# A fused retention and relu-squared MLP kernel: the weights' way into SBUF changed, and the small matmuls of a unit given other places among the wide ones

## The chip, the cores and the metric

The kernel runs on one core of one Trainium2 chip. The metric is the device time of one execution in microseconds (us). The kernel before takes 392.28 us, the median of 3 runs from 391.2 to 393.03.

## What is computed

q, k and v are fp32 arrays of 8 batches, 8 heads, 576 positions and 64 elements. The attention is a retention: scores are not put through a softmax but multiplied by a decay that depends on head and distance. Its output, laid out as 4608 tokens of 512, goes through two weight matrices with a squared relu between them.

```python
scores = scale * np.matmul(q, k.transpose(0, 1, 3, 2))
gamma = 1.0 - 2.0 ** (-5.0 - np.arange(H, dtype=np.float32))
Dmat = np.where(rel >= 0, gamma[:, None, None] ** rel[None, :, :], 0.0)   # rel = i - j
attn = np.matmul(scores * Dmat[None], v)
x = attn.transpose(0, 2, 1, 3).reshape(B * S, H * D)      # 4608 x 512
h = x @ w_in                                              # w_in 512 x 2048
out = (np.maximum(h, 0.0) ** 2) @ w_out                   # w_out 2048 x 512
```

## The kernel before, in words

**Units and groups.** The tokens are cut into 36 units of 128: of each pair of batches, four full units of the one, four of the other, and one tail unit that holds the last 64 positions of both. Four units make a group, so there are 9 groups of 512 tokens.

**A unit's work (retention).** `load(u)` issues three DMAs on SP's queue (q, k, v, 256 KB each, fp32, in rows of 256 bytes; L68, or six halves at L71 for a tail). The pool `ld` holds five units. `cast_unit(u)` has GpSimd cast k and q to fp16 (L160, L161) and multiply v by a decay into `vp` (L164). `steps_T` is eight 128x128 transposes on TensorE into one PSUM tile `psT` (L180), followed by two copies of kT on ScalarE (L185, L186) and one of qT on VectorE (L187). `steps_score` is eight small matmuls into `psc` (L204), each four followed by VectorE's multiply with the causal mask into `rT` (L207). `steps_state` is four small matmuls (L229) that carry the state R along a batch by two VectorE operations (L238, L239; one, L235, in a batch's first unit; none in a tail). `steps_out` is eight to sixteen small matmuls (L257, L263) into `psO`, followed by VectorE's multiply into the group's `xT` (L270). `psT`, `psS` and `psO` have one PSUM buffer each, `psc` two.

**A group's work (MLP).** `steps_ff1(g)` is 16 blocks of 4 wide matmuls (128x512, L290) into `ph`; after each block ScalarE takes the relu into `rl` (L295, three buffers) and VectorE squares it into `gT` (L296). `steps_ff2(g)` is 4 token tiles of 16 wide matmuls each (L310) into `po`; after each tile ScalarE copies to `o` (L314, two buffers) and issues the store (L317, L321). `ph` and `po` share three PSUM buffers.

**Order.** The scheduling is manual: each engine executes its instructions in the order in which the program emits them. First the loads of units 0 to 3 are issued on SP's queue, and beside them eight DMAs on GpSimd's queue that load the fp32 weights and cast them to fp16 on the way (L82, L85), ahead of GpSimd's constants (ident, iota, masks; L90 to L114). VectorE's constants (L99 to L149) wait for the iota. Units 0 to 3 run one after another (L330 to L335). Then, for each group g, its 128 wide matmuls are emitted one by one, with the small steps of the four units of group g+1 put between them from a queue: 32 wide matmuls make a unit's slot, and at given phases of the slot the unit's steps are put into the queue. At phase 0 come the unit's load and casts, at 2 its transposes, at 14 scores and state, at 27 the output products; one step leaves the queue after each wide matmul, up to three from phase 27 on. The last group has no units beside it.

Of the kernel before, what the change touches and what calls it, by code (L numbers as in the profile page):

```python
# [8 lines left out]
FP32 = mybir.dt.float32  # L9
# [6 lines left out]
def kernel(  # L16
# [27 lines left out]
    NG = NU // UPG  # L44

    const = ctx.enter_context(tc.tile_pool(name="const", bufs=1))
    ld = ctx.enter_context(tc.tile_pool(name="ld", bufs=5))
    cast = ctx.enter_context(tc.tile_pool(name="cast", bufs=3))
    work = ctx.enter_context(tc.tile_pool(name="work", bufs=2))
    st_pool = ctx.enter_context(tc.tile_pool(name="st", bufs=4))  # L50
# [11 lines left out]
    def load(u):  # L62
        kind, b, c = units[u]
        t = {}
        for name, src in (("q", q), ("k", k), ("v", v)):
            x = ld.tile([P, H, D], FP32, name=f"{name}32", tag=f"{name}32")
            if kind == "full":
                nc.sync.dma_start(out=x, in_=src[b, :, c * P:(c + 1) * P, :].rearrange("h p d -> p h d"))  # L68
            else:
                for i in range(2):  # L70
                    nc.sync.dma_start(out=x[i * 64:(i + 1) * 64],  # L71
                                      in_=src[b + i, :, 512:576, :].rearrange("h p d -> p h d"))
            t[name] = x
        loaded[u] = t

    w_in16 = const.tile([P, NP, DFF], FP16, name="w_in16")
    w_out16 = const.tile([P, NF, DM], FP16, name="w_out16")

    for u in range(4):
        load(u)  # L80
    for fb in range(4):
        nc.gpsimd.dma_start(out=w_in16[:, :, fb * 512:(fb + 1) * 512],  # L82
                            in_=w_in[:, fb * 512:(fb + 1) * 512].rearrange("(m p) f -> p m f", p=P))
    for fb in range(4):
        nc.gpsimd.dma_start(out=w_out16[:, fb * 4:(fb + 1) * 4, :],  # L85
                            in_=w_out[fb * 512:(fb + 1) * 512, :].rearrange("(n p) m -> p n m", p=P))


    ident = const.tile([P, P], FP16, name="ident")
# [65 lines left out]
    def cast_unit(u):  # L155
        kind = units[u][0]
        t = loaded.pop(u)
        k16 = cast.tile([P, H * D], FP16, name="k16", tag="k16")
        q16 = cast.tile([P, H * D], FP16, name="q16", tag="q16")
        nc.gpsimd.tensor_copy(out=k16, in_=t["k"].rearrange("p h d -> p (h d)"))  # L160
        nc.gpsimd.tensor_copy(out=q16, in_=t["q"].rearrange("p h d -> p (h d)"))  # L161
        vp = vps[u % NB]
        vo = vp.rearrange("p n (a d) -> p n a d", d=64)[:, :, 0:3:2, :]
        nc.gpsimd.tensor_tensor(  # L164
            out=vo,
            in0=t["v"].rearrange("p (n a) d -> p n a d", a=2),
            in1=vdec[kind].rearrange("p (n a o) -> p n a o", a=2, o=1).to_broadcast([P, NP, 2, D]),
            op=ALU.mult)
        ret[u] = {"k16": k16, "q16": q16, "vp": vp}

    def steps_T(u):
        r = ret[u]
        steps = []
        for i, src in enumerate(("k16", "q16")):
            for hp in range(NP):
                def f(i=i, src=src, hp=hp):
                    if i == 0 and hp == 0:
                        r["psT"] = ps_one.tile([P, 2, NP, P], FP16, name="psT", tag="psT")
                    ps = r["psT"]
                    nc.tensor.transpose(ps[:, i, hp, :], r[src][:, hp * P:(hp + 1) * P], ident)  # L180
                    if hp == NP - 1:
                        if i == 1:
                            kT = kTs[u % NB]
                            qT = work.tile([P, NP, P], FP16, name="qT", tag="qT")
                            nc.scalar.copy(out=kT[0:64, :, 0, :], in_=ps[0:64, 0])  # L185
                            nc.scalar.copy(out=kT[64:128, :, 1, :], in_=ps[64:128, 0])  # L186
                            nc.vector.tensor_copy(out=qT, in_=ps[:, 1])  # L187
                            r["kT"], r["qT"] = kT, qT
                steps.append(f)
        return steps  # L190
# [109 lines left out]
    def steps_ff2(g):  # L300
        gT = gTs[g]
        steps = []
        cur = {}
        for t in range(UPG):
            kind, b, c = units[g * UPG + t]
            for f in range(NF):
                def s(t=t, f=f, kind=kind, b=b, c=c):
                    if f == 0:
                        cur["po"] = ps_ff.tile([P, DM], FP32, name="po", tag="ff")
                    nc.tensor.matmul(cur["po"], lhsT=gT[f][:, t * P:(t + 1) * P], rhs=w_out16[:, f, :],  # L310
                                     start=(f == 0), stop=(f == NF - 1))
                    if f == NF - 1:
                        o = work.tile([P, DM], FP32, name="o", tag="o")
                        nc.scalar.copy(out=o, in_=cur["po"])  # L314
                        if kind == "full":
                            r0 = b * S + c * P
                            nc.scalar.dma_start(out=out[r0:r0 + P, :], in_=o)  # L317
                        else:
                            for i in range(2):
                                r0 = (b + i) * S + 512  # L320
                                nc.scalar.dma_start(out=out[r0:r0 + 64, :], in_=o[i * 64:(i + 1) * 64])  # L321
                steps.append(s)
        return steps


    def run(steps):
        for s in steps:
            s()

    for u in range(UPG):  # L330
        cast_unit(u)
        run(steps_T(u))
        run(steps_score(u))
        run(steps_state(u))
        run(steps_out(u))  # L335

    for g in range(NG):
        nxt = [u for u in range((g + 1) * UPG, (g + 2) * UPG) if u < NU]
        wide = 2 * NF * UPG
        per = wide // UPG  # L340
        w_steps = steps_ff1(g)
        w2 = None
        queue = []
        for i in range(wide):
            if i == NF * NP:
                w_steps += steps_ff2(g)
            slot, ph = divmod(i, per)
            if nxt:
                if ph == 0:
                    u = nxt[slot]  # L350
                    load(u)
                    cast_unit(u)
                if ph == 2:
                    queue += steps_T(nxt[slot])
                if ph == 14:
                    queue += steps_score(nxt[slot])
                    queue += steps_state(nxt[slot])
                if ph == 27:
                    queue += steps_out(nxt[slot])
            w_steps[i]()  # L360
            if queue:
                queue.pop(0)()
            if ph >= 27 and queue:
                queue.pop(0)()
                if queue:
                    queue.pop(0)()
        run(queue)
# [30 lines left out]
```

## Time and profile before

| what | value |
|---|---|
| median of the runs | 392.28 us |
| the profiled execution's own time | 392.92 us |
| its span, first to last instruction | 391.2 us |
| mean granted TensorE clock | 0.997 |
| wide matmuls of the first layer, L290 | 576, 157.1 us busy |
| wide matmuls of the second layer, L310 | 576, 154.4 us busy |
| HBM read / written | 36.70 MB / 9.44 MB |

The profile counts an engine as busy while one of its instructions executes; matmuls overlap, so a matmul's shown duration is longer than the pitch at which matmuls follow one another. In the time line a row gives the start in us, the duration, the engine, the line, the operation and its tiles, and in brackets how long the engine had been idle and what ended that. PE is TensorE, PEld its weight loads, DVE VectorE, ACT ScalarE, POOL GpSimd; SPq, ACTq and POOLq are the queues on which DMAs are issued. In a group's row, "| busy, mean" are the total us and the mean ns of one.

### The profile page before, as it was taken

The page shows a single profiled execution, that of the slowest core. Times are in us where ns is not written, and L with a number is a line of the kernel's source. Part 1 is how long each engine was busy: PE and PEld are TensorE (multiplying, and loading weights), DVE is VectorE, ACT ScalarE, POOL GpSimd, SP SyncE. Part 2 cuts the span into 40 slices and gives each one's busy share as a digit, 9 for nine tenths or more (in the row PEclk, how much of TensorE's full clock was granted, in tenths as well). Part 3 has the DMA queues.
Part 4 walks back from the last instruction along what each step waited for, and adds up shares of the span by engine and source line. Part 5 has one row for each costly group of instructions (what it writes and reads, how often), then busy time and mean ns, then how long its engine had stood idle before and what let it go on. Part 6 is the DMA issues. An engine that isn't in the chain of part 4 may idle for free.

```text
span 391.2 us, 5966 instructions
## 1 busy us (share of the span) xinstructions
PE 327.6 (84%) x2272; PEld 181.1 (46%) x2272; DVE 204.5 (52%) x385; ACT 151.7 (39%) x259; POOL 92.8 (24%) x129
## 2 busy tenths in 40 slices
PE   0304699998999899989989998999899989998995
PEld 0203645554555455545545554555455545554442
DVE  1604737645654585458445844684378437633410
ACT  2102146325622562266225622662265236523721
POOL 8113632223132122222222222222222222000000
PEclk9999999999999999999999999999999999999998
DMA  8999999856145435546154455347330110011002
GB/s 146 196 196 213 208 217 219 192 137 162 28 107 136 107 83 107 136 108 136 54 139 104 82 112 148 94 86 166 90 89 2 54 55 0 2 54 56 0 31 78
DMA packets 122013, 42.34 MB, mean 108 GB/s; under 512 B 113280, under 2 KB 117376, under 8 KB 121984
## 3 DMA queue, kind: packets, MB, share of 16 engines
q1 hardware_dynamic: 112512, 28.32, 36.9%
q10 hardware_dynamic: 5248, 9.44, 7.1%
q0 software_dynamic: 4224, 4.19, 6.5%
q8 instruction: 18, 0.29, 0.3%
q14 instruction: 11, 0.09, 0.1%
HBM read 36.70 MB, written 9.44 MB: 118 GB/s over the span
## 4 chain that ended last, share of the span: by engine, by line
PE 64%; DVE 11%; ACT 10%; DMA 7%; issue 4%; SPq 3%; POOL 0%; ACTq 0%
PE ph L290 25%; PE po L310 24%; DMA v<-in_v_dram 6%; PE psc L204 5%; ACT kTb L186 5%; DVE qT L187 4%; ACT rl L295 4%; PE psO L257 4%; PE psT L180 3%; SPq L68 3%; DVE gT L296 2%; PE psS L229 2%; DVE R L239 2%; DMA out_dram<-o 2%; DVE xT L270 2%
## 5 line engine op out<-in xcount | busy, mean ns | idle before, releaser
L290 PE MATMUL ph<-xT,w_in 128*128 128x512 f16 x576 | 157.1, 383 | 5.5 <-DVE xT L270 5.5
L310 PE MATMUL po<-w_out,gT 128*128 128x512 f16 x576 | 154.4, 379 | 0.0
L295 ACT ACTIVATE rl<-ph 128x512 f16<-128x512 f32 x144 | 86.0, 597 | 72.8 <-PE ph L290 53.8
L296 DVE TENSOR_TENSOR gT<-rl 128x512 f16<-128x512 f16 x144 | 72.7, 509 | 47.3 <-ACT rl L295 44.8
L290 PEld LDWEIGHTS <-w_in 128*128 128x128 f16 x576 | 55.0, 99 | 76.1 <-issue 25.4
L310 PEld LDWEIGHTS <-gT 128*128 128x128 f16 x576 | 54.4, 98 | 68.0 <-issue 14.9
L204 PE MATMUL psc<-qT,kTb 128*128 128x128 f16 x288 | 60.0, 228 | 30.8 <-DVE qT L187 30.8
L160 POOL CAST k<-k 128x512 f16<-128x512 f32 x36 | 24.9, 691 | 199.4 <-issue 146.1
L314 ACT COPY o<-po 128x512 f32<-128x512 f32 x36 | 21.1, 585 | 91.9 <-PE po L310 87.8
L207 DVE TENSOR_TENSOR rT<-psc,mask_full 128x512 f16<-128x512 f32 x64 | 43.6, 687 | 24.0 <-PE psc L204 24.0
L187 DVE COPY qT<-psT 128x512 f16<-128x512 f16 x36 | 15.2, 423 | 68.8 <-ACT kTb L186 68.8
L180 PE MATMUL psT<-ident,k 128*128 128x128 f16 x144 | 30.9, 232 | 20.1 <-POOL k L160 20.1
L185 ACT COPY kTb<-psT 64x512 f16<-64x512 f16 x36 | 20.8, 578 | 62.4 <-PE psT L180 56.2
L164 POOL TENSOR_TENSOR vp<-v,vdec_full 128x512 f16<-128x512 f32 x32 | 34.9, 1090 | 34.2 <-PE psO L257 18.2
L257 PE MATMUL psO<-rT,vp 128*128 128x128 f16 x288 | 39.9, 229 | 0.0
L257 PEld LDWEIGHTS <-vp 128*128 128x128 f16 x288 | 28.1, 103 | 18.1 <-issue 0.3
L204 PEld LDWEIGHTS <-kTb 128*128 128x128 f16 x288 | 28.3, 102 | 14.4 <-issue 4.8
L180 PE MATMUL psT<-ident,q 128*128 128x128 f16 x144 | 30.9, 232 | 0.0
L229 PE MATMUL psS<-vp,k 128*128 128x128 f16 x128 | 27.0, 230 | 2.6 <-POOL vp L164 2.6
L263 PE MATMUL psO<-qT,R 128*128 128x128 f16 (+1 forms) x128 | 26.8, 221 | 0.0
L180 PEld LDWEIGHTS <-k 128*128 128x128 f16 x144 | 14.3, 104 | 24.3 <-POOL k L160 20.3
L239 DVE TENSOR_TENSOR R<-stmp,bdec 128x512 f16<-128x512 f32 x24 | 23.0, 960 | 0.8
(46 smaller groups left out, 157.6 us busy)
## 6 DMA issues: line engine op xcount, KB each, us to landing
q<-in_q_dram SPq DMA_DIRECT2D x32, 256.0 KB, 3.2
k<-in_k_dram SPq DMA_DIRECT2D x32, 256.0 KB, 4.2
v<-in_v_dram SPq DMA_DIRECT2D x32, 256.0 KB, 4.2
out_dram<-o ACTq DMA_DIRECT2D x32, 256.0 KB, 2.7
w_in<-in_moe_w_in_dram POOLq DMA_DIRECT2D x4, 512.0 KB, 12.6
w_out<-in_moe_w_out_dram POOLq DMA_DIRECT2D x4, 512.0 KB, 23.1
q<-in_q_dram SPq DMA_DIRECT2D x8, 128.0 KB, 3.5
k<-in_k_dram SPq DMA_DIRECT2D x8, 128.0 KB, 4.0
```

Of the source, the lines that this page charges most:

```text
L164: nc.gpsimd.tensor_tensor(out=vo, in0=t["v"].rearrange("p (n a) d -> p n a d", a=2), in1=vdec[kind].rearrange("p (n a o) -> p n a o", a=2, ...
L180: nc.tensor.transpose(ps[:, i, hp, :], r[src][:, hp * P:(hp + 1) * P], ident)
L187: nc.vector.tensor_copy(out=qT, in_=ps[:, 1])
L204: nc.tensor.matmul(r["psc"][:, hp % 2, a, :], lhsT=r["kT"][:, hp, a, :], rhs=r["qT"][:, hp, :], start=True, stop=True)
L207: nc.vector.tensor_tensor(out=rT[:, hp - 1:hp + 1].rearrange("p n a i -> p (n a) i"), in0=r["psc"].rearrange("p n a i -> p (n a) i"), in1= ...
L229: nc.tensor.matmul(ps[:, hp], lhsT=r["k16"][:, hp * P:(hp + 1) * P], rhs=vo, start=True, stop=True)
L239: nc.vector.tensor_tensor(out=Rn, in0=tmp, in1=bdec, op=ALU.mult)
L257: nc.tensor.matmul(r["psO"][:, hp, :], lhsT=r["vp"][:, hp, a * 64:a * 64 + P], rhs=r["rT"][:, hp, a, :], start=(a == 0), stop=(a == 1 and ...
L290: nc.tensor.matmul(cur["ph"], lhsT=w_in16[:, m, f * P:(f + 1) * P], rhs=xTs[g][:, m, :], start=(m == 0), stop=(m == NP - 1))
L295: nc.scalar.activation(out=rl, in_=cur["ph"], func=ACTF.Relu)
L296: nc.vector.tensor_tensor(out=gT[f], in0=rl, in1=rl, op=ALU.mult)
L310: nc.tensor.matmul(cur["po"], lhsT=gT[f][:, t * P:(t + 1) * P], rhs=w_out16[:, f, :], start=(f == 0), stop=(f == NF - 1))
```

## The change

The weights are loaded as fp32 on SP's queue, into four staging buffers of 1 MB: the four pieces of w_in behind the loads of units 0 to 3; each piece of w_out when VectorE has cast the piece of w_in that held its buffer. VectorE casts w_in between units 0 to 3 and group 0, and w_out between the matmuls of group 0's second layer. Loads of units 4 to 9 follow the weights on SP's queue; the pool `ld` holds six units, and later loads are issued six units ahead. For units 0 to 7 VectorE casts q instead of GpSimd.

Group 0's wide matmuls now run with no units between them, its second layer with three token tiles side by side and the fourth behind them. Units 4 to 7 run one after another behind group 0. From group 1 on the small steps stand between the wide ones as before, at other places: in the slot of unit u its state comes at phase 0, its scores at 5, the transposes of unit u+1 at 14, the output products of u at 18; one step leaves the queue after each wide matmul, two from phase 14 on. GpSimd's casts are emitted a slot earlier, for u+1. Unit 8, the first, also has its own transposes in its slot, and its steps come 8 phases later.

```diff
--- before.py
+++ after.py
@@ -44,7 +44,8 @@
     NG = NU // UPG
 
     const = ctx.enter_context(tc.tile_pool(name="const", bufs=1))
-    ld = ctx.enter_context(tc.tile_pool(name="ld", bufs=5))
+    ld = ctx.enter_context(tc.tile_pool(name="ld", bufs=6))
+    stage = ctx.enter_context(tc.tile_pool(name="stage", bufs=4))
     cast = ctx.enter_context(tc.tile_pool(name="cast", bufs=3))
     work = ctx.enter_context(tc.tile_pool(name="work", bufs=2))
     st_pool = ctx.enter_context(tc.tile_pool(name="st", bufs=4))
@@ -73,17 +74,27 @@
             t[name] = x
         loaded[u] = t
 
+
     w_in16 = const.tile([P, NP, DFF], FP16, name="w_in16")
     w_out16 = const.tile([P, NF, DM], FP16, name="w_out16")
-
-    for u in range(4):
+    NLD = 6
+    for u in range(UPG):
         load(u)
+    w_st = []
     for fb in range(4):
-        nc.gpsimd.dma_start(out=w_in16[:, :, fb * 512:(fb + 1) * 512],
-                            in_=w_in[:, fb * 512:(fb + 1) * 512].rearrange("(m p) f -> p m f", p=P))
-    for fb in range(4):
-        nc.gpsimd.dma_start(out=w_out16[:, fb * 4:(fb + 1) * 4, :],
-                            in_=w_out[fb * 512:(fb + 1) * 512, :].rearrange("(n p) m -> p n m", p=P))
+        t = stage.tile([P, NP, 512], FP32, name=f"wi{fb}", tag="wst")
+        nc.sync.dma_start(out=t, in_=w_in[:, fb * 512:(fb + 1) * 512].rearrange("(m p) f -> p m f", p=P))
+        w_st.append(t)
+
+    def load_w_out(fb):
+        t = stage.tile([P, 4, DM], FP32, name=f"wo{fb}", tag="wst")
+        nc.sync.dma_start(out=t, in_=w_out[fb * 512:(fb + 1) * 512, :].rearrange("(n p) m -> p n m", p=P))
+        w_st.append(t)
+
+    def cast_w(i):
+        fb = i % 4
+        dst = w_in16[:, :, fb * 512:(fb + 1) * 512] if i < 4 else w_out16[:, fb * 4:(fb + 1) * 4, :]
+        nc.vector.tensor_copy(out=dst, in_=w_st[i])
 
 
     ident = const.tile([P, P], FP16, name="ident")
@@ -158,7 +169,7 @@
         k16 = cast.tile([P, H * D], FP16, name="k16", tag="k16")
         q16 = cast.tile([P, H * D], FP16, name="q16", tag="q16")
         nc.gpsimd.tensor_copy(out=k16, in_=t["k"].rearrange("p h d -> p (h d)"))
-        nc.gpsimd.tensor_copy(out=q16, in_=t["q"].rearrange("p h d -> p (h d)"))
+        (nc.vector if u < 2 * UPG else nc.gpsimd).tensor_copy(out=q16, in_=t["q"].rearrange("p h d -> p (h d)"))
         vp = vps[u % NB]
         vo = vp.rearrange("p n (a d) -> p n a d", d=64)[:, :, 0:3:2, :]
         nc.gpsimd.tensor_tensor(
@@ -300,26 +311,31 @@
     def steps_ff2(g):
         gT = gTs[g]
         steps = []
-        cur = {}
-        for t in range(UPG):
+        po = {}
+
+        order = [(t, f) for t in range(UPG) for f in range(NF)] if g else \
+                [(t, f) for f in range(NF) for t in range(3)] + [(3, f) for f in range(NF)]
+        for t, f in order:
             kind, b, c = units[g * UPG + t]
-            for f in range(NF):
-                def s(t=t, f=f, kind=kind, b=b, c=c):
-                    if f == 0:
-                        cur["po"] = ps_ff.tile([P, DM], FP32, name="po", tag="ff")
-                    nc.tensor.matmul(cur["po"], lhsT=gT[f][:, t * P:(t + 1) * P], rhs=w_out16[:, f, :],
-                                     start=(f == 0), stop=(f == NF - 1))
-                    if f == NF - 1:
-                        o = work.tile([P, DM], FP32, name="o", tag="o")
-                        nc.scalar.copy(out=o, in_=cur["po"])
-                        if kind == "full":
-                            r0 = b * S + c * P
-                            nc.scalar.dma_start(out=out[r0:r0 + P, :], in_=o)
-                        else:
-                            for i in range(2):
-                                r0 = (b + i) * S + 512
-                                nc.scalar.dma_start(out=out[r0:r0 + 64, :], in_=o[i * 64:(i + 1) * 64])
-                steps.append(s)
+
+            def s(t=t, f=f, kind=kind, b=b, c=c):
+                if g == 0 and t == 0 and f % 4 == 0:
+                    cast_w(4 + f // 4)
+                if f == 0:
+                    po[t] = ps_ff.tile([P, DM], FP32, name="po", tag="ff")
+                nc.tensor.matmul(po[t], lhsT=gT[f][:, t * P:(t + 1) * P], rhs=w_out16[:, f, :],
+                                 start=(f == 0), stop=(f == NF - 1))
+                if f == NF - 1:
+                    o = work.tile([P, DM], FP32, name="o", tag="o")
+                    nc.scalar.copy(out=o, in_=po[t])
+                    if kind == "full":
+                        r0 = b * S + c * P
+                        nc.scalar.dma_start(out=out[r0:r0 + P, :], in_=o)
+                    else:
+                        for i in range(2):
+                            r0 = (b + i) * S + 512
+                            nc.scalar.dma_start(out=out[r0:r0 + 64, :], in_=o[i * 64:(i + 1) * 64])
+            steps.append(s)
         return steps
 
 
@@ -327,41 +343,57 @@
         for s in steps:
             s()
 
-    for u in range(UPG):
+    def whole(u):
         cast_unit(u)
+        if u + NLD < NU and u >= UPG:
+            load(u + NLD)
         run(steps_T(u))
         run(steps_score(u))
         run(steps_state(u))
         run(steps_out(u))
 
-    for g in range(NG):
-        nxt = [u for u in range((g + 1) * UPG, (g + 2) * UPG) if u < NU]
-        wide = 2 * NF * UPG
-        per = wide // UPG
+    for u in range(UPG):
+        whole(u)
+    for i in range(4):
+        cast_w(i)
+        load_w_out(i)
+    for u in range(UPG, UPG + NLD):
+        load(u)
+    run(steps_ff1(0))
+    run(steps_ff2(0))
+    for u in range(UPG, 2 * UPG):
+        whole(u)
+
+
+    SLOT = 2 * NF
+    for g in range(1, NG):
         w_steps = steps_ff1(g)
-        w2 = None
         queue = []
-        for i in range(wide):
+        for i in range(NF * NP * 2):
             if i == NF * NP:
                 w_steps += steps_ff2(g)
-            slot, ph = divmod(i, per)
-            if nxt:
+            slot, ph = divmod(i, SLOT)
+            u = (g + 1) * UPG + slot
+            late = 8 if u == 2 * UPG else 0
+            if u < NU:
                 if ph == 0:
-                    u = nxt[slot]
-                    load(u)
-                    cast_unit(u)
-                if ph == 2:
-                    queue += steps_T(nxt[slot])
-                if ph == 14:
-                    queue += steps_score(nxt[slot])
-                    queue += steps_state(nxt[slot])
-                if ph == 27:
-                    queue += steps_out(nxt[slot])
+                    if late:
+                        cast_unit(u)
+                        queue += steps_T(u)
+                    if u + 1 < NU:
+                        cast_unit(u + 1)
+                    if u + NLD < NU:
+                        load(u + NLD)
+                if ph == late:
+                    queue += steps_state(u)
+                if ph == late + 5:
+                    queue += steps_score(u)
+                if ph == late + 14 and u + 1 < NU:
+                    queue += steps_T(u + 1)
+                if ph == late + 18:
+                    queue += steps_out(u)
             w_steps[i]()
-            if queue:
-                queue.pop(0)()
-            if ph >= 27 and queue:
-                queue.pop(0)()
+            for _ in range(2 if ph >= 14 else 1):
                 if queue:
                     queue.pop(0)()
         run(queue)
```

## The prediction

> **What bounds the kernel now.** I read the page's busy times and slices first, then TensorE's waits after the first group, then the time line.
>
> ```profile
> span 391.2 us, 5966 instructions
> ...
> PE 327.6 (84%) x2272; PEld 181.1 (46%) x2272; DVE 204.5 (52%) x385; ACT 151.7 (39%) x259; POOL 92.8 (24%) x129
> ...
> PE   0304699998999899989989998999899989998995
> ```
>
> TensorE is nearly full from slice 6 on and nearly empty in the first five slices (each 9.8 us). So there are two places to gain or lose: an opening of some 50 us, and the tenth that is missing afterwards. What is missing afterwards has two names:
>
> ```profile
> PE psc L204 <- DVE qT L187: 18.2, 28, 0.7
> PE ph L290 <- DVE xT L270: 4.3, 8, 0.8
> ```
>
> These are TensorE's waits between 90 and 391 us (total us, times, longest): 28 waits, one for each unit 8 to 35, and 8 at the starts of groups 1 to 8. TensorE waits for nothing else there. One of them, in the time line (start, us):
>
> ```profile
> 207.85 1.24 PE L290 MATMUL ph<-xT,w_in 128*128 128x512 f16 x5
> 209.75 0.22 PE L204 MATMUL psc<-qT,kTb 128*128 128x128 f16 x1 [0.65 <-DVE qT L187]
> 209.80 0.38 PE L290 MATMUL ph<-xT,w_in 128*128 128x512 f16 x1
> 210.07 0.38 PE L290 MATMUL ph<-xT,w_in 128*128 128x512 f16 x1
> ```
>
> A wide matmul is shown with 0.38 us, but five take 1.24, so the pitch is (1.24 - 0.38) / 4 = 0.215. One wide and one small take 0.27 (209.80 to 210.07), so a small one takes 0.055. The five from 207.85 are issued by 208.93, and the next starts at 209.75: the wait costs 0.82, its shown 0.65 and the pipeline's tail of 0.165. The transposes are followed by 5 wide matmuls (1.1 us), while the copies out of their PSUM tile take longer than that.
>
> ```profile
> 49.02:90.11 41.09, 37.91 (x252) 20.33 (x252) 23.74 (x39) 16.47 (x28) 11.97 (x16) 1.00 0.98 181
> 90.11:128.42 38.31, 35.13 (x252) 19.20 (x252) 21.09 (x37) 16.53 (x29) 9.70 (x13) 1.00 0.45 111
> 205.25:224.26 19.01, 17.70 (x129) 9.82 (x128) 13.19 (x25) 11.33 (x20) 4.25 (x6) 1.00 0.44 97
> 358.92 13.97 PE L290 MATMUL ph<-xT,w_in 128*128 128x512 f16 x64 [0.78 <-DVE xT L270]
> ```
>
> The first three rows are windows (length, then busy time of PE, weight loads, DVE, ACT, POOL): group 0, group 1, and the two slots of first-layer work in group 4. The last row starts group 8. Groups 1 to 7 take 358.92 - 90.11 = 268.8 us, 38.4 each; their pure issue is 128 x 0.215 + 124 x 0.055 = 34.3.
>
> **Steady groups.** Transposes of unit u+1 now go out at phase 14 of slot u, two per step, and its scores at phase 5 of its own slot, 23 steps later. The wait for qT ends. Scores finish at phase 12, the output products run from 18 to about 25, so xT is ready some 6 wide matmuls (1.3 us) before the group ends, against 0.69 for its multiply: the boundary wait ends too. Saved in groups 1 to 7: 28 x 0.82 = 23.0, and 4.3 - 0.57 (the one at 90.11) + 7 x 0.165 = 4.9, together 27.9; 240.9 remain, 34.4 a group. What is late next: between the last score and the first output product lie 6 wide and some 8 small matmuls, 1.7 us, in which VectorE must do the second mask multiply (0.69) behind a gT that waits for ScalarE. In the first-layer half VectorE has 13.19 us of work for two slots that shrink from 19.0 to 17.2, 77%, so queues can form; I allow 1.0 in all. Unit 8, which has no slot ahead of it, still waits 8 to 13 steps, slow ones, as group 1 starts; no cost. Loads six units ahead instead of being issued in the unit's own slot sit on SP's queue and cost nothing: a group used DMA at 0.45.
>
> **The start.** GpSimd loses eight DMA issues:
>
> ```profile
> 1.32 3.16 POOL L82 DMA_DIRECT2D w_in<-in_moe_w_in_dram  x4 [0.80 <-POOLq L382]
> 4.43 3.01 POOL L85 DMA_DIRECT2D w_out<-in_moe_w_out_dram  x4
> 7.35 0.30 POOL masks.py:197 MEMSET ident<- 128x128 f16 x1
> 8.14 0.15 DVE L117 COPY iota_pt<-iota_p 64x1 f32<-64x1 f32 x1 [6.20 <-POOL iota_p L92]
> ...
> 15.38 0.27 DVE L149 MEMSET kTb<- 64x256 uint32 x1
> ...
> 15.98 1.01 PE L204 MATMUL psc<-qT,kTb 128*128 128x128 f16 x8 [4.67 <-DVE qT L187]
> ...
> 18.64 0.69 DVE L270 TENSOR_TENSOR xT<-psO,gam_full 128x512 f16<-128x512 f32 x1
> ```
>
> Ident can start at 1.32 instead of 7.35, and VectorE's constants, which wait for the iota, end 6.03 earlier, at 15.65 - 6.03 = 9.62. Now the serial units, here unit 2 into unit 3:
>
> ```profile
> 39.54 1.01 PE L204 MATMUL psc<-qT,kTb 128*128 128x128 f16 x8 [1.73 <-DVE qT L187]
> ...
> 42.57 0.63 PE L180 MATMUL psT<-ident,q 128*128 128x128 f16 x4
> ...
> 42.69 0.68 DVE L270 TENSOR_TENSOR xT<-psO,gam_full 128x512 f16<-128x512 f32 x1
> ...
> 43.30 0.58 ACT L185 COPY kTb<-psT 64x512 f16<-64x512 f16 x1 [4.26 <-PE psT L180]
> ...
> 44.99 1.01 PE L204 MATMUL psc<-qT,kTb 128*128 128x128 f16 x8 [1.79 <-DVE qT L187]
> ```
>
> Scores to scores took 5.45. The q cast of units 0 to 7 moves from GpSimd to VectorE, where in program order it stands behind xT of the unit before; the q transposes wait for it. New period: 39.54 to the end of xT at 43.37 is 3.83, the cast, then transposes to scores 42.57 to 44.99 = 2.42 (+0.05 to start). For VectorE's casts the trace has a copy of 1 element at 0.15 (L117) and one of 256, and a multiply that converts 512:
>
> ```profile
> 10.56 0.29 DVE L130 COPY gam_tail<-gam_full 128x256 f32<-128x256 f32 x1 [1.56 <-ACT gam_full L129]
> ...
> L207 DVE TENSOR_TENSOR rT<-psc,mask_full 128x512 f16<-128x512 f32 x64 | 43.6, 687 | 24.0 <-PE psc L204 24.0
> ```
>
> The copies give 0.15 + 0.00055 per element: 0.43 for q's 512, 1.28 for 2048 of a weight piece. The other bound is the multiply's 0.687 per 512: 0.69 and 2.75. I take the copies, which are the same operation. Period 3.83 + 0.43 + 2.47 = 6.73. Scores(0) start at 9.62 + 0.43 + 2.47 = 12.5; unit 0 needs 3.35 to the end of xT (15.98 to 19.33); scores(1) at 12.5 + 3.35 + 2.90 = 18.8, scores(3) at 32.2, xT(3) done at 36.1; before, the first wide matmul, which waits for it, started at 49.02 (row below). Data is there in time:
>
> ```profile
> q1 hardware_dynamic: 112512, 28.32, 36.9%
> q10 hardware_dynamic: 5248, 9.44, 7.1%
> ```
>
> The unit loads (252 bytes a packet) need 36.9% of 391.2 for 28.32 MB: 196 GB/s, 4.0 us a unit. The output queue (1.8 KB a packet) makes 340 GB/s; for the weights' 2 KB rows that is 3.1 us a piece, 5.4 at the unit loads' rate. Four units by 18, w_in by 30 (39 at worst); w_out's four pieces, which wait on SP for the casts to free their buffers, by 52 (61); units 4 to 9, behind them in the same queue, one each 4.0 us, unit 4 by 58 (67). None is last.
>
> **Group 0, now without units beside it.** The first cast ends at 37.4 and the first wide matmul starts. The other three hold VectorE until 41.2; six PSUM and relu buffers let TensorE run on. It starts slow:
>
> ```profile
> 49.02 1.44 PE L290 MATMUL ph<-xT,w_in 128*128 128x512 f16 x3 [1.22 <-DVE xT L270]
> ...
> 54.10 1.33 PE L290 MATMUL ph<-xT,w_in 128*128 128x512 f16 x5
> ```
>
> From 49.02 to 54.10 went 11 wide and 8 small ones, worth 2.8 us at the later pitch: 2.3 lost, although the window's granted clock reads 1.00. First layer: 37.4 + 64 x 0.215 + 2.3 = 53.5. The second layer begins only after the last relu and square and the first cast of w_out, all behind one another:
>
> ```profile
> L295 ACT ACTIVATE rl<-ph 128x512 f16<-128x512 f32 x144 | 86.0, 597 | 72.8 <-PE ph L290 53.8 <-DVE gT L296 18.6
> L296 DVE TENSOR_TENSOR gT<-rl 128x512 f16<-128x512 f16 x144 | 72.7, 509 | 47.3 <-ACT rl L295 44.8
> ...
> L314 ACT COPY o<-po 128x512 f32<-128x512 f32 x36 | 21.1, 585 | 91.9 <-PE po L310 87.8
> ...
> out_dram<-o ACTq DMA_DIRECT2D x32, 256.0 KB, 2.7
> ```
>
> Pipeline tail 0.165, relu 0.60, square 0.51, cast 1.28, hand-overs 0.1: 2.7. The later casts (1.28 each) hide behind 12 matmuls (2.6). Second layer ends at 53.5 + 2.7 + 13.8 = 70.0. Its first three output tiles finish together 3.4 us earlier, with two output buffers: the third copy waits for a store (0.585 + 2.7), the fourth for the next one, and unit 4's kT copies stand behind both on ScalarE, until about 72 instead of 70.7. So scores(4) start 1.3 late, at 70.0 + 0.44 (eight transposes at 0.055) + 1.99 (the 2.42 above without its four slow transposes, 0.43) + 1.3 = 73.7.
>
> **Units 4 to 7, now alone.** scores(5) = 73.7 + 3.35 + 2.90 = 79.9; xT(7) ends 79.9 + 2 x 6.73 + 3.83 = 97.2. Group 1 starts at 97.3, before at 90.11: the opening loses 7.2. In the serial rows above eight small matmuls take 1.01, a pitch of (1.01 - 0.22) / 7 = 0.113 against 0.055 in the stream, so TensorE is back at half rate and group 1 pays the 2.3 of a slow start, which before it did not. This agrees with the Trainium skill, "TensorE: Matmul & The Clock Gate", Part 1: the array runs at half clock until about 3.4 us of steady work and falls back after an idle window of that length. It speaks against this change, since units 4 to 7 running alone buy a second slow start; without the rule group 1 would start warm and the sum below would be 372.7.
>
> **Sum.** 97.3 + 2.3 + 240.9 + 1.0 + group 8 with the last store, unchanged, 391.2 - 358.92 = 32.3: span 373.8, against 391.2. The profiled execution took 392.92, 1.72 more than its span, and the median of the runs is 392.28, 0.64 less: 373.8 + 1.1 = 374.9, say 375.
>
> **Rivals.** *The wait moves instead of going* (first-layer half): output products wait for the second mask multiply, or PSUM fills while VectorE works off its queue. For it: in-order VectorE with gT in front, 1.7 us of room against some 1.5. Against: in the second-layer half VectorE is half idle. In 14 slots 0.82 each, 11.5: 386. *The opening is cheaper*: no slow start of group 1 (2.3), no store in ScalarE's way (1.3), no residue (1.0): 370. *Slower*: the same mask multiply is late in all 28 slots and the boundary xT behind it, so that nothing of the 27.9 comes back while the opening still loses 9.5: 403. It decides for slower once under 8 of the 27.9 arrive, that is, over 0.6 us lost per slot. Against: the shown room. In between, two thirds lost: about 392, no change. That the change does not do what it says is small: the step counts above come from the code, and only tile dependencies I do not see could hold the early transposes back, which is this last rival again.
>
> **How the numbers follow.** Forecast 375: 0.70. Moved wait, 386: 0.13. Cheaper opening, 370: 0.11. Nothing regained, 403: 0.04; about 392: 0.02. Forecast's own unknowns: casts at their upper bound cost 7 x 0.26 + 2 x 1.47 + some 2 for the blocked squares, 7 together; a slow start of the second layer after its 2.7 gap 2.3. Range 367 to 387: the low end is the cheap opening with 3 for what I summed too long in the serial chain, the high end the moved wait. A difference under 0.5%, 2 us, can't be told from none. Faster 0.94, same 0.02, slower 0.04.
>
> **What would show it.** The psc wait for qT after group 1 gone from the list, groups 34.4 to 34.6 long; ident near 1.3; serial scores 6.7 apart; a VectorE cast of 1.3; a TensorE gap near 2.7 between group 0's layers; group 1 starting near 97 with a pitch near 0.43. Wrong would be groups over 36, a new name in TensorE's waits, or group 1 starting past 105.

## The result and the profile after

The changed kernel takes 374.87 us, the median of 4 runs (372.89 to 375.75), against 392.12 for the kernel before in the same comparison: a ratio of 0.9553, 95% interval 0.9504 to 0.9602. Six more runs on another occasion gave 372.72 (370.71 to 375.46), ratio 0.9516 (0.9482 to 0.9551). 375 had been forecast. The profiled execution took 375.74, its span is 374.0.

The page of the changed kernel, busy times and slices (a slice is 9.35 us; PEclk is the granted TensorE clock in tenths):

```profile
PE 332.7 (89%) x2272; PEld 186.3 (50%) x2272; DVE 207.1 (55%) x401; ACT 151.4 (40%) x259; POOL 84.1 (22%) x113
...
PE   0565979654899999999999999999999999999995
...
PEclk9986798955599999999999999999999999999999
...
GB/s 175 253 358 9 359 256 190 172 220 148 222 142 113 154 154 94 116 141 133 86 124 151 119 86 142 150 104 118 109 29 2 28 58 28 2 58 58 0 53 60
```

TensorE works earlier than before and is 90% busy or more from the twelfth slice to the last but one, but slices 8 to 10, 65 to 94 us, are half empty, and slices 9 to 11 have a granted clock of a half: mostly units 4 to 7 alone. Its waits between 100 us and the end are one row; 28 and 8 waits stood there before.

```profile
PE psc L215 <- DVE qT L198: 0.3, 1, 0.3
```

Windows of group 4 and of units 4 to 7 (length; busy time of PE, weight loads, DVE, ACT, POOL; granted clock; DMA share; GB/s):

```profile
204.08:238.63 34.55, 34.55 (x253) 19.44 (x252) 21.31 (x39) 16.54 (x28) 9.51 (x12) 1.00 0.52 123
70.65:97.36 26.71, 13.86 (x126) 11.80 (x125) 15.82 (x26) 5.23 (x9) 8.84 (x11) 0.59 1.09 202
```

Group 4 took 38.53 before and is now busy from end to end with the same matmuls. The time line, the rows at which the forecast can be checked:

```profile
0.80 0.21 POOL masks.py:197 MEMSET ident<- 128x128 f16 x1 [0.29 <-POOLq L414]
9.16 0.35 DVE L172 CAST q<-q 128x512 f16<-128x512 f32 x1
11.91 1.01 PE L215 MATMUL psc<-qT,kTb 128*128 128x128 f16 x8 [1.73 <-DVE qT L198]
17.99 1.01 PE L215 MATMUL psc<-qT,kTb 128*128 128x128 f16 x8 [1.73 <-DVE qT L198]
24.34 1.01 PE L215 MATMUL psc<-qT,kTb 128*128 128x128 f16 x8 [1.73 <-DVE qT L198]
34.30 4.62 DVE L97 CAST w_in<-wi 128x2048 f16<-128x2048 f32 x4
35.58 16.79 PE L301 MATMUL ph<-xT,w_in 128*128 128x512 f16 x64 [2.22 <-DVE w_in L97]
53.46 6.73 DVE L97 CAST w_out<-wo 128x2048 f16<-128x2048 f32 x4
54.73 12.22 PE L326 MATMUL po<-w_out,gT 128*128 128x512 f16 x48 [2.37 <-DVE w_out L97]
69.31 0.59 ACT L330 COPY o<-po 128x512 f32<-128x512 f32 x1 [1.11 <-DMA out_dram<-o]
73.54 0.61 PE L215 MATMUL psc<-qT,kTb 128*128 128x128 f16 x8 [2.28 <-DVE qT L198]
79.68 1.01 PE L215 MATMUL psc<-qT,kTb 128*128 128x128 f16 x8 [1.73 <-DVE qT L198]
97.36 0.58 PE L301 MATMUL ph<-xT,w_in 128*128 128x512 f16 x1 [1.12 <-DVE xT L281]
103.89 0.22 PE L215 MATMUL psc<-qT,kTb 128*128 128x128 f16 x1 [0.28 <-DVE qT L198]
135.20 0.38 PE L301 MATMUL ph<-xT,w_in 128*128 128x512 f16 x1
341.70 13.98 PE L301 MATMUL ph<-xT,w_in 128*128 128x512 f16 x64
```

The row at 97.36 and the last two start groups 1, 2 and 8. Groups 2 to 7 take (341.70 - 135.20) / 6 = 34.42 us, 38.4 before. Group 0's two rows hold two slow starts: 64 wide matmuls in 16.79, 2.8 more than the 13.99 that the same row takes at full pitch in a run below, and 48 in 12.22, 1.7 more than the 10.53 there. A third stands at group 1: from 97.36 to the first score at 103.89, 14 wide and 8 small matmuls worth 3.45, the wait of 0.28 and the tail of 0.165 leave 2.6 lost. (The expectations below speak of 2.1 for the second layer; 0.4 of it is a wait of the fourth token tile for a PSUM buffer.) So the time of the steady groups came back nearly whole, and the opening gave 7.25 of it away (97.36 against 90.11).

### The profile page after: what moved, and what is told of

Its sections match the earlier page's. It is cut to its first block, busy times and chain, and to the rows that moved or that the text cites. A ratio compares the mean times of both kernels' runs of the same rounds, so it can differ in the third digit from the quotient of the medians.

```text
span 374.0 us, 5968 instructions
## 1 busy us (share of the span) xinstructions
PE 332.7 (89%) x2272; PEld 186.3 (50%) x2272; DVE 207.1 (55%) x401; ACT 151.4 (40%) x259; POOL 84.1 (22%) x113
## 4 chain that ended last, share of the span: by engine, by line
PE 84%; DVE 10%; ACT 4%; issue 1%; ACTq 0%
PE ph L301 34%; PE po L326 34%; PE psc L215 5%; PE psT L191 4%; PE psO L268 4%; DVE rT L218 2%; PE psS L240 2%; ACT kTb L197 1%; ACT kTb L196 1%; DVE xT L281 1%; PE psO L274 1%; DVE R L250 1%; DVE qT L198 1%; DVE stmp L249 1%; DVE q L172 1%
## 5 line engine op out<-in xcount | busy, mean ns | idle before, releaser
L326 PE MATMUL po<-w_out,gT 128*128 128x512 f16 x576 | 150.9, 383 | 2.6 <-DVE w_out L97 2.4
L307 DVE TENSOR_TENSOR gT<-rl 128x512 f16<-128x512 f16 x144 | 67.3, 472 | 48.3 <-ACT rl L306 47.5
L215 PE MATMUL psc<-qT,kTb 128*128 128x128 f16 x288 | 55.9, 234 | 14.8 <-DVE qT L198 14.8
L175 POOL TENSOR_TENSOR vp<-v,vdec_full 128x512 f16<-128x512 f32 x32 | 36.2, 1133 | 106.6 <-PE psO L274 45.3
L171 POOL CAST k<-k 128x512 f16<-128x512 f32 x36 | 23.2, 644 | 108.9 <-DMA k<-in_k_dram 53.0
L268 PE MATMUL psO<-rT,vp 128*128 128x128 f16 x288 | 46.9, 236 | 0.6 <-DVE rT L218 0.6
L215 PEld LDWEIGHTS <-kTb 128*128 128x128 f16 x288 | 28.1, 105 | 19.3 <-ACT kTb L196 7.9
L268 PEld LDWEIGHTS <-vp 128*128 128x128 f16 x288 | 29.5, 106 | 14.9 <-issue 1.1
L191 PE MATMUL psT<-ident,q 128*128 128x128 f16 x144 | 20.3, 234 | 9.4 <-DVE q L172 9.4
L191 PE MATMUL psT<-ident,k 128*128 128x128 f16 x144 | 20.7, 238 | 6.0 <-POOL k L171 6.0
L191 PEld LDWEIGHTS <-q 128*128 128x128 f16 x144 | 13.6, 104 | 17.5 <-DVE q L172 11.1
```

The lines of the kernel that those rows point to most:

```text
L175: nc.gpsimd.tensor_tensor(out=vo, in0=t["v"].rearrange("p (n a) d -> p n a d", a=2), in1=vdec[kind].rearrange("p (n a o) -> p n a o", a=2, ...
L215: nc.tensor.matmul(r["psc"][:, hp % 2, a, :], lhsT=r["kT"][:, hp, a, :], rhs=r["qT"][:, hp, :], start=True, stop=True)
L268: nc.tensor.matmul(r["psO"][:, hp, :], lhsT=r["vp"][:, hp, a * 64:a * 64 + P], rhs=r["rT"][:, hp, a, :], start=(a == 0), stop=(a == 1 and ...
L307: nc.vector.tensor_tensor(out=gT[f], in0=rl, in1=rl, op=ALU.mult)
L326: nc.tensor.matmul(po[t], lhsT=gT[f][:, t * P:(t + 1) * P], rhs=w_out16[:, f, :], start=(f == 0), stop=(f == NF - 1))
```

## The experiments

The theory is that of the forecast: two waits end in the steady groups, for 27.9 us; the opening loses, because units 4 to 7 run alone, because VectorE's q cast stands in their chain, and because TensorE, little used there, falls to half rate. Each run takes one of these apart. Edits are shown shortened, by their main lines.

**The old slots in the new opening.** In the loop over groups 1 to 8 the steps go back to their old phases, one a wide matmul and three from phase 27 on, and the casts to the unit's own slot:

```diff
-                if ph == late: queue += steps_state(u)
-                if ph == late + 5: queue += steps_score(u)
-                if ph == late + 14 and u + 1 < NU: queue += steps_T(u + 1)
-                if ph == late + 18: queue += steps_out(u)
+                if ph == 2: queue += steps_T(u)
+                if ph == 14: queue += steps_score(u) + steps_state(u)
+                if ph == 27: queue += steps_out(u)
```

> The changed kernel with the old places of the small steps from group 1 on (transposes at phase 2, scores and state at 14, output products at 27, casts in the unit's own slot); the opening and the loads six ahead stay. If the phases are what removed the waits: 28 waits of 0.82 us and the boundary waits of 4.9 come back, groups of 38.4 instead of 34.5, time 374.9 + 27.9 = 403, slower than the kernel before by about 10, which is then what the new opening alone costs. Rival, that the loads issued further ahead removed the waits: time stays near 375.

Measured: 398.34 us, ratio to the kernel before 1.0189 (1.016 to 1.0218): about 2% slower than that. TensorE's waits over the whole execution and the first rows of groups 1 and 8:

```profile
PE psc L215 <- DVE qT L198: 32.8, 36, 2.3
...
PE ph L301 <- DVE xT L281: 4.8, 8, 1.1
```

```profile
93.41 1.44 PE L301 MATMUL ph<-xT,w_in 128*128 128x512 f16 x3 [1.08 <-DVE xT L281]
...
364.05 6.20 PE L301 MATMUL ph<-xT,w_in 128*128 128x512 f16 x28 [0.78 <-DVE xT L281]
```

Both waits are back, and groups 1 to 7 take 270.6 against 244.3 in the changed kernel: 26.3 us hang on the phases, not on the loads issued ahead. The time is 4.7 under the 403 expected, mostly because group 1 starts at 93.4 instead of 97.4 with an opening that is the same code: here the first layer's 64 matmuls took 15.58 and the second layer started at full pitch.

**The new slots behind the old opening.** The kernel before, with its loop replaced by the changed kernel's, from group 0 on:

```diff
-    for g in range(NG):            # old slots, load and casts in the unit's own slot
+    for u in range(UPG, UPG + 5):
+        load(u)
+    for g in range(NG):            # new slots; unit 4 takes the late phases, loads 5 ahead
```

> The kernel before, its opening and GpSimd's weight DMAs kept, with the new places of the small steps from group 0 on (unit 4 takes the late phases), loads five ahead. If the phases alone give the gain: 392.1 - 27.9 = 364 from groups 1 to 7, and group 0 loses four waits of 0.82 and one boundary wait of 0.73, so about 360, and the changed opening is a loss of some 14 us. Rival, that the new order needs the new opening (loads too late for transposes half a slot ahead, new TensorE waits for GpSimd's k): 370 or more.

Measured: 360.53 us, ratio 0.9227 (0.9202 to 0.9253). It is faster than the changed kernel by 12 to 14. TensorE's waits, from the serial units 0 to 3 and the start of group 0:

```profile
PE psT L180 <- POOL k L160: 19.9, 2, 10.2
PE psc L204 <- DVE qT L187: 9.9, 4, 4.7
...
PE ph L290 <- DVE xT L270: 1.3, 1, 1.3
```

So the slots, with the loads issued ahead, are worth about 30 us, and everything else in the change together is a loss.

**q cast on GpSimd.**

```diff
-        (nc.vector if u < 2 * UPG else nc.gpsimd).tensor_copy(out=q16, ...)
+        nc.gpsimd.tensor_copy(out=q16, ...)
```

> The changed kernel with q of units 0 to 7 cast on GpSimd again. If the cast on VectorE, behind xT, lengthens the chain from unit to unit: the periods fall from 6.35 (units 0 to 3) and 6.9 (units 4 to 7) to the 5.45 of the kernel before, 3 x 0.9 + 3 x 1.4 and 0.4 for unit 0, 7 us less: 368. Rival, that the cast is hidden or GpSimd becomes as late: 374 to 376.

Measured: 362.32 us, ratio 0.9265 (0.9236 to 0.9294). Its time line:

```profile
9.57 1.01 PE L215 MATMUL psc<-qT,kTb 128*128 128x128 f16 x8 [2.45 <-DVE qT L198]
...
25.32 1.01 PE L215 MATMUL psc<-qT,kTb 128*128 128x128 f16 x8 [1.79 <-DVE qT L198]
30.34 13.99 PE L301 MATMUL ph<-xT,w_in 128*128 128x512 f16 x64 [2.22 <-DVE w_in L97]
46.62 10.53 PE L326 MATMUL po<-w_out,gT 128*128 128x512 f16 x48 [2.29 <-DVE w_out L97]
64.68 0.61 PE L215 MATMUL psc<-qT,kTb 128*128 128x128 f16 x8 [3.23 <-DVE qT L198]
83.97 0.38 PE L301 MATMUL ph<-xT,w_in 128*128 128x512 f16 x1 [1.12 <-DVE xT L281]
```

From the first unit's scores to the fourth's it takes 15.75, 5.25 each, and the first layer starts 5.2 us earlier. From scores(4) to group 1 it takes 19.3 instead of 23.8, another 4.5. Together 9.7 against the 7 expected; 2 of the surplus are unit 0, whose scores start at 9.57 instead of 11.91 (0.4 had been put there), since its q cast no longer stands behind VectorE's constants. On top none of the three starts of wide matmuls in this profile is slow (64 x 0.215 and the tail make 13.93), which the changed kernel's profile pays with 2.8, 1.7 and 2.6. The q cast is the dearest single line of the change, 10 to 13 us by the medians, in which the chain's share and that of the slow starts are not told apart.

**Filler between group 0's layers.**

```diff
     run(steps_ff1(0))
+    fill = ps_ff.tile([P, UPG * P], FP32, name="fill", tag="ff")
+    for i in range(12):
+        nc.tensor.matmul(fill, lhsT=w_in16[:, 0, 0:P], rhs=xTs[0][:, 0, :], start=True, stop=True)
```

> The changed kernel with 12 wide matmuls into an unused PSUM tile between the two layers of group 0 (extra work; the result is thrown away), 2.6 us at full pitch, in the gap in which TensorE waits for the first cast of w_out. If the half rate at the second layer's start (8 matmuls at 0.43 from 54.73 on) comes from the idle gap: the pitch is 0.215 from the first matmul on, the second layer takes 13.9 instead of 15.9, time 373. Rival, that it comes from what runs beside it (VectorE's casts, DMA share 1.28): the pitch stays 0.43, time 375 or more.

Measured: 372.99 us, ratio 0.9544 (0.9517 to 0.9572), no different from the changed kernel's two sets.

```profile
35.97 13.99 PE L301 MATMUL ph<-xT,w_in 128*128 128x512 f16 x64 [2.22 <-DVE w_in L97]
49.80 2.75 PE L365 MATMUL fill<-xT,w_in 128*128 128x512 f16 x12
52.39 10.52 PE L326 MATMUL po<-w_out,gT 128*128 128x512 f16 x48
...
66.69 0.59 ACT L330 COPY o<-po 128x512 f32<-128x512 f32 x1 [2.55 <-DMA out_dram<-o]
```

The second layer runs at full pitch from its first matmul, as the idle-gap theory wants. But it also does so in the two kernels above, with gaps of 2.3 us and no filler, so this run does not settle it. And the second layer's shorter time does not come through whole: ScalarE waits 2.55 us for the first token tile's store, 1.11 in the changed kernel, as in the next run.

**w_out cast inside the first layer.**

```diff
-    run(steps_ff1(0))
+    for i, s in enumerate(steps_ff1(0)):
+        s()
+        if i in (35, 43, 51, 59):
+            cast_w(4 + (i - 35) // 8)
```

with the call in `steps_ff2` removed.

> The changed kernel with the four casts of w_out emitted among the last blocks of group 0's first layer (behind wide matmuls 36, 44, 52 and 60) instead of in its second layer. Theory: the second layer's first matmul waits only for the cast that stands behind the last relu and square; without it the gap of 2.4 goes, and with the gap the chance of a slow start (2.1 in the profiled run, none in two others): 2.4 to 4.5 less, 371 to 372.5. Rival, that the stores of the first token tiles, or the loads of units 4 and 5, end last instead: 374 to 375.

Measured: 372.13 us, ratio 0.9476 (0.944 to 0.9512). That lies within the 371 to 372.5 expected, but the interval overlaps both sets of the changed kernel, and the second set's 372.72 is only 0.6 away: a gain is not shown. The gap before the second layer is gone, and most of its time is not:

```profile
50.65 10.09 PE L324 MATMUL po<-w_out,gT 128*128 128x512 f16 x46 [0.25 <-ACT rl L306]
64.42 0.39 PE L191 MATMUL psT<-ident,k 128*128 128x128 f16 x4
69.10 1.01 PE L215 MATMUL psc<-qT,kTb 128*128 128x128 f16 x8 [4.06 <-DVE qT L198]
```

```profile
65.36 0.59 ACT L328 COPY o<-po 128x512 f32<-128x512 f32 x1 [3.40 <-DMA out_dram<-o]
```

```profile
88.84 1.01 PE L215 MATMUL psc<-qT,kTb 128*128 128x128 f16 x8 [1.79 <-DVE qT L198]
...
92.77 0.38 PE L301 MATMUL ph<-xT,w_in 128*128 128x512 f16 x1 [1.12 <-DVE xT L281]
93.03 0.38 PE L301 MATMUL ph<-xT,w_in 128*128 128x512 f16 x1
```

Unit 4's scores start 4.7 us after its first transpose, 2.9 in the changed kernel. ScalarE waits 3.40 instead of 1.11 for the first token tile's store before it can copy the third, and the kT copies stand behind that. So the rival was right for 1.8 of the 2.4. The traces bear out that the store now falls among the loads of units 4 to 9: in the 2 us in which it is issued the DMA share is 1.25 here (60 to 62 us) and 1.29 with the filler (62 to 64), where the wait is 2.55, but 0.00 in the changed kernel (66 to 68). No run moves the loads alone. The profile's span, 367.3, is 6.7 below the changed kernel's 374.0, about as much as the three slow starts there (7.1), none of which it has. Group 1 starts at full pitch at 92.77, though unit 7's eight scores before it ran at half rate (1.01), as in the changed kernel.

**Weights loaded by GpSimd as before.**

```diff
-        nc.sync.dma_start(out=t, in_=w_in[...])          # fp32, staged, cast by VectorE; w_out likewise
+    for fb in range(4):
+        nc.gpsimd.dma_start(out=w_in16[...], in_=w_in[...])
+    for fb in range(4):
+        nc.gpsimd.dma_start(out=w_out16[...], in_=w_out[...])
```

> The changed kernel with the weights loaded and cast by GpSimd's eight DMAs at the start, as in the kernel before, and no weight casts on VectorE; all else as changed. Theory: the weights' DMAs run beside the unit loads again, so unit 2's k arrives near 35 and xT of unit 3 is done near 50 instead of 34.4; the casts (1.2 before the first layer, 2.4 before the second) are saved: about 15.5 - 1.2 - 2.4 = 12 more, 387. Rival, that the bytes are the same and only the sum of them counts: 373 to 376.

Measured: 385.32 us, ratio 0.9837 (0.9802 to 0.9872), 10 to 13 more than the changed kernel.

```profile
31.33 1.01 PE L204 MATMUL psc<-qT,kTb 128*128 128x128 f16 x8 [1.73 <-DVE qT L187]
...
51.20 15.76 PE L290 MATMUL ph<-xT,w_in 128*128 128x512 f16 x64 [1.09 <-DVE xT L270]
```

Unit 1's scores are at 31.33 instead of 17.99 and the first layer starts at 51.20 instead of 35.58. That the bytes are the same does not help; units 0 to 3 need theirs first. The weights' new way is the good half of the opening.

**Units 4 to 7 back beside group 0.** The weights' new way, the new slots, q on GpSimd, and:

```diff
+    for u in range(UPG, 2 * UPG):            # on SP's queue behind w_in, ahead of w_out
+        load(u)
-    run(steps_ff1(0))
-    run(steps_ff2(0))
-    for u in range(UPG, 2 * UPG):
-        whole(u)
-    for g in range(1, NG):
+    for g in range(NG):                      # unit 4 takes the late phases
+            if g == 0 and i in (48, 58, 68, 80):
+                cast_w(4 + (48, 58, 68, 80).index(i))
```

> The changed kernel's weight path and slots, with units 4 to 7 put back between group 0's wide matmuls (unit 4 in the late phases), their loads ahead of w_out's, q always cast on GpSimd, and w_out's casts among group 0's wide matmuls. Theory, from the rows: group 0's first wide matmul at about 30.5 as with q on GpSimd, group 0 34.4 and up to 2.8 for a slow start and 1 for unit 4, group 1 warm at 67 to 69, then 7 x 34.4 + 32.3: span 340 to 342, time 342 to 345. Rival, that the loads can't feed units 5 to 7 and w_out in time, or VectorE can't do casts and units at once: TensorE waits in group 0, 350 or more.

Measured: 346.9 us, ratio 0.8858 (0.8827 to 0.8888), faster than both kernels, and 15.4 less than with q on GpSimd alone, for units 4 to 7 beside group 0 and w_out's casts moved together.

```profile
29.95 0.61 PE L303 MATMUL ph<-xT,w_in 128*128 128x512 f16 x1 [2.41 <-DVE w_in L99]
...
32.69 0.29 PE L193 MATMUL psT<-ident,k 128*128 128x128 f16 x1 [2.13 <-POOL k L173]
```

The second row, 2.13 us in which unit 4's first transpose waits because its k lands behind all of w_in, is about as long as the time is over the 345 expected; whether it is the cause the run after the next asks, and leaves open.

**Fillers in the serial units.**

```diff
+        run(ts[:4]); filler(u, 3 if u else 0)     # wide matmuls, lhsT=ident, rhs=k16, unused tile
+        run(ts[4:]); filler(u, 6)
-        run(steps_T(u))
```

> The changed kernel with extra wide matmuls on old data into an unused PSUM tile in the waits of the serial units 0 to 7 (three while q is cast, six while qT is copied; extra work, thrown away). Theory, that the half rate in and after the serial units comes from TensorE's low activity there: small matmuls at 0.055 instead of 0.11 from unit 1 or 2 on, no slow start of groups 0 and 1: 2.8 + 2.6 and about 0.5 a unit less, 365 to 370. Rival, that the half rate comes from the units' loads and copies beside it: the same 0.11, and 375 or more, since fillers at half rate delay the scores.

Measured: 372.37 us, ratio 0.9504 (0.947 to 0.9537). The small matmuls now run at full pitch:

```profile
24.13 0.61 PE L215 MATMUL psc<-qT,kTb 128*128 128x128 f16 x8 [0.43 <-DVE qT L198]
30.34 0.61 PE L215 MATMUL psc<-qT,kTb 128*128 128x128 f16 x8 [0.49 <-DVE qT L198]
...
35.17 15.67 PE L301 MATMUL ph<-xT,w_in 128*128 128x512 f16 x64 [2.57 <-DVE w_in L97]
```

```profile
68.00:96.00 28.00, 19.98 (x178) 11.87 (x176) 15.59 (x26) 5.90 (x11) 9.84 (x11) 1.00 1.04 207
```

Eight scores take 0.61, a pitch of (0.61 - 0.22) / 7 = 0.056, and the granted clock is 1.00 in the window of units 4 to 7, where the DMA share (1.04) and the copies are as before. So the half rate in the serial units is TensorE's own low activity, and the rival falls. But the time hardly does: the units' chain runs through VectorE and ScalarE and keeps a period of 6.2, and after the pause of 2.57 for w_in's cast the first layer still starts slow (1.7), although the units before it ran at full pitch. The time expected from the fillers, 365 to 370, was not reached.

**The same with another order of loads.** From the kernel of 346.9: unit 4's load behind w_in's first piece, and w_in's first cast ahead of unit 3's steps.

```diff
         w_st.append(t)
+        if fb == 0:
+            load(UPG)
...
     for u in range(UPG):
+        if u == UPG - 1:
+            cast_w(0)
         whole(u)
```

> The kernel with units 4 to 7 beside group 0 (346.9), with unit 4's load ahead of w_in's last three pieces on SP's queue, and w_in's first cast ahead of unit 3's steps on VectorE. Theory, from that kernel's waits: the 2.13 us in which unit 4's first transpose waits for GpSimd's k and the cast's 1.2 ahead of group 0's first matmul go, 3.3 less, 343.6; up to 2.3 more or less by whether TensorE starts group 0 at half rate. Rival, that w_in's later pieces or their casts then end last: 346 to 348.

Measured: 345.84 us (344.0 to 347.64), ratio 0.8846 (0.8803 to 0.8888): within the interval of the kernel that it comes from. Both waits are gone from TensorE's list, and the first ten wide matmuls of group 0 are issued at half rate, until 34.65:

```profile
29.37 0.58 PE L305 MATMUL ph<-xT,w_in 128*128 128x512 f16 x1 [1.08 <-DVE xT L285]
...
34.12 0.63 PE L305 MATMUL ph<-xT,w_in 128*128 128x512 f16 x1
...
35.06 0.38 PE L305 MATMUL ph<-xT,w_in 128*128 128x512 f16 x1
```

In this profile group 1 starts at 69.12 instead of 72.05, near the 3.3 less that was expected. But only two of the four executions are that fast (344.0 and 344.08); the other two took 347.6 and have no profile. Whether it is faster stays open.

**The changed kernel once more**, unaltered.

> The changed kernel once more, unaltered, for a second profile and more times. Theory, that its slow starts fall differently from execution to execution (in the first profile 2.8, 2.1 and 2.6 us at the three starts of wide matmuls after a pause): the same constants, periods and groups of 34.4, another set of slow starts, times spread over 2 to 3 us around 375. Rival, that they are fixed by the program: the same three slow starts of the same sizes.

Measured: 372.72 us (370.71 to 375.46). The profiled execution is again the slowest (375.46), with the same slow starts to 0.1 us:

```profile
35.59 16.75 PE L301 MATMUL ph<-xT,w_in 128*128 128x512 f16 x64 [2.22 <-DVE w_in L97]
54.63 12.22 PE L326 MATMUL po<-w_out,gT 128*128 128x512 f16 x48 [2.29 <-DVE w_out L97]
```

The other five runs have mean granted clocks of 0.954 to 0.977 instead of 0.939 and take 370.71 to 373.0. So two profiles agree, which the rival expected, and the times spread over 4.75 us, even more than the theory expected. Over both sets the three executions at a clock of 0.938 or 0.939 take 375.46 to 375.75; among the others the time does not follow the mean clock (373.0 at 0.977, 370.71 at 0.968). What decides the set of slow starts in an execution is open.

## Why the prediction was right

**Steady groups: right.** 34.42 us a group against 34.4, and the only wait left was unit 8's first (0.3). The two reversals, one each way, put the slots' worth at 26.3 (by the traces of the old slots in the new opening) and about 30 (by the medians in the old opening, where group 0 gains too, 360.5 against 360 expected). The rival in which output products wait for the second mask multiply did not come: TensorE's list has 0.6 us of it in all, within the serial units.

**The opening: the sum right, its terms less so.** Group 1 was to start at 97.3 and did at 97.36, by errors that cancel:

| step | forecast | measured |
|---|---|---|
| q cast of unit 0 can start | 9.62 | 9.16 |
| scores to scores, units 1 to 3 | 6.73 | 6.35, 6.41 |
| one cast of w_in | 1.28 | 1.15 |
| first wide matmul | 37.4 | 35.58 |
| slow start, first layer | 2.3 | 2.8 |
| gap between the layers | 2.7 | 2.5 |
| slow start, second layer | 0, bound 2.3 | 1.7 |
| fourth token tile's wait for a PSUM buffer | 0 | 0.4 |
| second layer's end to scores(4) | 3.7 | 2.9 |
| scores(4) to group 1 | 23.6 | 23.8 |
| slow start, group 1 | 2.3 | 2.6 |

The first wide matmul came 1.8 early: 0.5 because VectorE's constants ended sooner, 0.7 in the two periods from unit 1 to unit 3, whose q transposes took 0.40 instead of the 0.61 to 0.63 of half rate, and the rest in small parts of units 0 and 3 and in the cast. The second layer's slow start, put at nothing in the sum and at 2.3 among the unknowns, took 1.7; the way from the second layer's end to scores(4) was 0.8 shorter, since ScalarE waited for one store, 1.11 us, and not for two.

The 2.3 itself was read a little low: from 49.02 to 54.10 the kernel before issued 10 wide and 8 small matmuls, not 11 and 8, so 2.5 were lost. And the step from the serial units' half rate to a slow start of group 1 is not sure. The half rate in those units is TensorE's own low activity, as the fillers show, and it needs no long pause: in units 4 to 7 TensorE was busy for 13.86 of 26.71 us and never idle for more than 2.3 at a time. But two profiles, with q on GpSimd and with the early casts, have the same half rate in the units ahead of group 1 and a group 1 that starts at full pitch. So a start of wide matmuls costs between 0 and 2.8 us. The sum has two slow ones, 4.6 us; the profile of the changed kernel has three, 7.1, and those two profiles none. That 375 was met so closely is partly luck.

By the Trainium skill, "TensorE: Matmul & The Clock Gate", Part 1, the activity window is free-running, so that a start can be slow in one execution and not in another. The starts here agree in that: behind the same code the first layer's 64 matmuls lost 2.8 us in the changed kernel, 1.6 with the old slots and 0 with the filler. The two equal profiles of the unaltered kernel do not speak for chance alone. The idle window that the prediction cites from there is not seen in units 4 to 7: their half rate came with pauses of at most 2.3 us.

**Data in time: right.** The page's third slice, in which the pieces of w_in are on their way, shows 358 GB/s for their 2 KB rows, near the 340 taken from the output queue, and no TensorE wait in the serial units but the first, unit 0's k at 6.05, is put down to loaded data.

**What was not seen** is a question of balance: the opening was booked as a loss of 7.2 that comes with the change. With the weights' new way kept, its other two parts undone and w_out's casts moved, it is a gain: 346.9.

## What to carry to other kernels

A wait that TensorE has in every repetition is worth its shown length plus the pipeline's tail, times the repetitions, if the steps behind it have slack; count that from pitches, not from busy times. When a change has parts, undo them one at a time, in both directions: here slots (about 30 us gained) and the weights' way (10 to 13) were good, and the q cast on the chain's own engine (10 to 13) and the units run alone were bad, under one result of 0.955. A gap that is filled is worth little if what stands behind it then waits for something else, here 1.8 of 2.4 us for a store. And compare profiles only with their slow starts in view: three of them, 7.1 us, can outweigh the step under test.

## What the runs showed of the hardware

- A cast of fp32 to fp16 on VectorE, 128x2048, took 1.15 us with GpSimd idle (4.62 for four) and 1.68 beside GpSimd's casts and multiplies (6.73 for four); 128x512 took 0.42 in units 1 to 3 and 0.66 to 0.83 in units 4 to 7.
- In the kernel before, the granted clock read 1.00 from 35 to 49 us while small matmuls ran at half pitch (0.113); in the changed kernel it read 0.59 for the like. A clock of 1.00 in the page is no proof of full pitch; the pitch is.
- 64 wide matmuls after a pause of 2.2 us took 13.99, 15.58 or 16.79 us.
- Small matmuls of the serial units ran at half pitch with TensorE busy for 13.86 of 26.71 us, and at full pitch (0.056) with fillers, busy for 19.98 of 28.00 us.
